# Attention beside a feed-forward layer: partial PV sums and the start of the other matmul groups

## The chip, the cores and the metric

The kernel runs on one core of one Trainium2 chip. The metric is the device time of one execution in microseconds. Three runs of the kernel before gave 674.62, 674.64 and 674.77 us; their median is 674.64 us.

## The reference

One input `x` of 2048 tokens by 640 features goes through a layer norm. Two branches then read the normalised tokens, and the output is the sum of the input and both branches:

```
xn = layernorm(x)
q = xn @ wq            # 32 heads of 20
k, v = xn @ wk, xn @ wv   # one head, shared by all 32
o = softmax(q k^T / sqrt(20)) @ v
h = relu(xn @ w1 + b1) ** 2     # 1536 wide
out = x + o @ wo + h @ w2 + b2
```

All tensors are bf16. By far the largest piece is the softmax: 32 heads by 2048 queries by 2048 keys of exponentials.

## The kernel before

**Tiling.** The 2048 queries are cut into four chunks of 512 and the 32 heads into eight groups of four, so that there are 32 blocks (line `NBLK`). A block has 16 key tiles of 128. A block and a key tile give four units, one for each head: a QK product of 20 rows by 128 keys by 512 queries that fills one PSUM bank. The four heads of a group use four different row strips of TensorE, so one batch of up to four QK matmuls runs side by side (line 1397).

**Two ways to an exponential.** ScalarE takes two or three units in one ACTIVATE of 1024 or 1536 columns (line 1678, tile PT). VectorE takes units one at a time (line 1777, tile pbx): it adds a constant, rounds to int16 and so makes an approximate exponential by bit pattern. A key tile that goes this way needs four such instructions and three copies of the result with an added phase of 32, 64 or 96; these are made by VectorE (line 1798) or in pieces by GpSimd (line 1860). A ScalarE tile then costs one step of the PV sum, a VectorE tile four.

**PV.** A step of PV is four matmuls of 32 output columns in four column strips (line 1991). All steps of a block add up in one PSUM bank. When the sum is complete, VectorE copies it to SBUF (line 2051), the softmax sum goes through three small DMAs, and the block is divided and packed for the output product.

**The other groups.** Feed-forward, query projection and output groups are sums in PSUM too, of 5 to 18 steps of four matmuls (line 1015, functions `groups` and `u_FFN`, `u_OUT`, `u_QP`). There are 48 feed-forward groups, 19 query groups and 32 output groups. Each has a place in units of blocks at which it is due. VectorE reads each result.

**PSUM.** There are eight banks. In most of the kernel banks 0 to 4 belong to ScalarE's units (three and two in turn), and banks 5, 6 and 7 (`MREG`, line 91) are shared by the open PV sum, the open group of the other kind, and VectorE's QK units. If none of the three is free for VectorE, bank 2 can be lent to it (lines 1485 to 1492), and then ScalarE's batch has two units in place of three.

**Order of the work.** The order of each engine's queue is made at build time by a list scheduler (class `Sched`, line 264). Streams (QK, exponentials, VectorE's tiles, PV, the other groups) offer their next instruction with a priority, and the scheduler issues by its own account of when engines and banks come free. A table `PLAN` (line 95) has 64 rows, one for each half block, with thresholds and with a seed; `pick` (line 1373) uses the seed to choose at some steps between small variants, as other lead times or one unit fewer. Everything on the chip then waits on semaphores in that fixed order.

**What sets the start of a PV sum and of a group.** `PVblk` (line 1937) runs the PV sum of one block. With `MX = 0` (line 186) it opens as soon as one step is ready (`SEG0 = 1`). For blocks 2 to 28 a sum may be cut once (`SEGS = 2`) where only one step is waiting, at least 8 are done and at least 8 are left (line 1983). The part is then added up in SBUF by `evict` (line 2022), its bank is given back, and the next part opens when 4 steps wait, or earlier if the buffers of exponentials fill up (`SEGR` PT slots of 24 or `SEGP` pbx buffers of 10). `due` (line 2163) lets a group of the other kinds start when it is one block late (`mlate`), or up to two blocks early (`mearly`) if no more than 4 PV steps are waiting (`mq`). It does not ask whether a PV sum is open.

Of the kernel before, what the change touches and what calls it, by code (L numbers as in the profile page):

```python
# [159 lines left out]
)]  # L160
PAAT = 24.7
PAQ = ()
NPX = 1
# [22 lines left out]
MX, MXL, MXP, MXE = 0, 1.0, 0, 1.0  # L186
# [19 lines left out]
PVEND = 0.5  # L206
# [3 lines left out]
PVU = 0.8  # L210
# [314 lines left out]
def bass_parallel_sum__grouped_kv_mqa__dense_activation_squared_relu__prompt_kernel(nc, A_x, A_wq, A_wk, A_wv, A_wo, B_x, B_w1, B_b1, B_w2, B_b2, out):  # L525
    es = ExitStack()
    with es:
# [77 lines left out]
        sc = Sched()  # L605
# [762 lines left out]
        def plan(name):  # L1368
            return spot[1][name]
# [937 lines left out]
```

## Time and profile before

| what | value |
|---|---|
| median of three runs | 674.64 us |
| profiled execution, its own time | 675.58 us |
| its span, first to last instruction | 673.8 us |
| TensorE clock granted | full over the whole span |
| ScalarE busy | 655.6 us, 97% |
| VectorE busy | 616.6 us, 92% |
| TensorE, pipelined ends modelled | 663.5 us, 98% |
| GpSimd busy | 464.1 us, 69% |
| DMA, mean | 45 GB/s |

The span is the time between the first and the last instruction of the trace, so the profiled execution has 1.8 us around it. A busy TensorE is not TensorE at its peak, since matmul ends overlap in the trace; the spacing of starts tells more. `PEld` are weight loads, which run beside the matmuls. The idle time in a row is that of the engine just before the instructions of that row, followed by what ended it.

### The profile page before, as it was taken

To read this page: it belongs to the slowest core of one execution; us is meant where nothing else is said; L and a number is where in the kernel's file an instruction comes from. 1 tells how busy PE (TensorE), PEld (TensorE's weight loads), DVE (VectorE), ACT (ScalarE), POOL (GpSimd) and SP (SyncE) were. 2 spreads that over 40 slices of the span, in tenths; PEclk is the share of its full clock that TensorE was granted. 3 is DMA by queue.
4 is the path that set the end of the run, shared out by engine and by line. 5 is a ranking of instruction groups with operands and counts; after the bars stand their busy time and mean duration, and the time that the engine had idled before them with its cause. 6 is when DMAs were issued, how large, how long until landed. Compare 5 with 4: busy or idle time off the path is not lost.

```text
span 673.8 us, 23427 instructions
## 1 busy us (share of the span) xinstructions
PE 663.5 (98%) x9828; PEld 225.5 (33%) x9828; DVE 616.6 (92%) x1114; ACT 655.6 (97%) x664; POOL 464.1 (69%) x808
## 2 busy tenths in 40 slices
PE   8999999999999999999999999999999999999998
PEld 6332222222223333332322333332233333333334
DVE  7988999999998898989999898889999998998897
ACT  6999999999999999999999999999999999999994
POOL 2657777867777777778878577776766777776700
PEclk9999999999999999999999999999999999999999
DMA  9441222311111111110111111120110011111001
GB/s 262 129 71 46 52 60 72 83 45 38 25 24 32 34 44 38 27 45 18 25 30 28 45 43 27 29 51 19 31 31 20 20 44 45 38 38 32 22 2 42
DMA packets 39914, 30.43 MB, mean 45 GB/s; under 512 B 22817, under 2 KB 34818, under 8 KB 39810
## 3 DMA queue, kind: packets, MB, share of 16 engines
q1 hardware_dynamic: 39810, 28.93, 18.2%
q8 instruction: 79, 1.29, 0.8%
q14 instruction: 25, 0.20, 0.1%
HBM read 11.49 MB, written 2.62 MB: 21 GB/s over the span
## 4 chain that ended last, share of the span: by engine, by line
PE 64%; ACT 19%; DVE 15%; DMA 1%; issue 1%; POOL 0%
PE ps L1991 24%; PE ps L1397 20%; PE ps L1015 19%; ACT PT L1678 19%; DVE pbx L1777 8%; DVE stats L743 2%; DVE pbx L1798 1%; DVE hT_tmp L1151 1%; DMA dn<-Tn 1%; DMA pbx<-in_A_x_dram 0%; DVE big L1159 0%; DVE Tn L2051 0%; DVE qpk L1106 0%; DVE OTs L2067 0%; DVE xnT L958 0%
## 5 line engine op out<-in xcount | busy, mean ns | idle before, releaser
L1678 ACT ACTIVATE PT<-ps 128x1024 bf16<-128x1024 f32 (+1 forms) x641 | 649.4, 1163 | 3.9 <-PE ps L1397 3.3
L1860 POOL INT64_ADD pbx<-pbx x767 | 445.3, 600 | 158.5 <-DVE pbx L1798 84.2
L1777 DVE TENSOR_SCALAR pbx<-ps 128x512 int16<-128x512 f32 x629 | 413.7, 686 | 40.4 <-PE ps L1397 37.1
L1397 PE MATMUL ps<-qT,kT 20*128 20x512 bf16 x2048 | 250.8, 384 | 3.5 <-DVE pbx L1777 2.0
L1991 PE MATMUL ps<-pbx,vp 128*32 128x512 bf16 x1896 | 174.4, 383 | 0.2 <-POOL pbx L1860 0.2
L1397 PEld LDWEIGHTS ps<-qT,kT 20*128 20x128 bf16 x2048 | 63.0, 91 | 241.6 <-ACT PT L1678 156.7
L1991 PE MATMUL ps<-PT,vx 128*32 128x512 bf16 x1416 | 135.9, 383 | 0.1
L1015 PE MATMUL ps<-xnT,w_sb 128*32 128x512 bf16 x960 | 72.9, 383 | 0.2
L1015 PE MATMUL ps<-w_sb,big 128*32 128x320 bf16 x1536 | 72.1, 301 | 0.1
L1798 DVE TENSOR_SCALAR pbx<-pbx 128x2048 int16<-128x2048 int16 x102 | 69.1, 689 | 0.3
L1991 PEld LDWEIGHTS ps<-pbx,vp 128*32 128x32 bf16 x1896 | 46.5, 95 | 56.5 <-issue 35.3
L1991 PE MATMUL ps<-pbx,vx 128*32 128x512 bf16 x632 | 61.2, 383 | 0.0
L1991 PEld LDWEIGHTS ps<-PT,vx 128*32 128x32 bf16 x1416 | 36.3, 95 | 42.5 <-issue 31.3
L1015 PEld LDWEIGHTS ps<-w_sb,big 128*32 128x32 bf16 x1536 | 34.1, 96 | 25.4 <-issue 17.9
L1151 DVE TENSOR_SCALAR hT_tmp<-ps,b1col 128x512 bf16<-128x512 f32 x48 | 35.6, 742 | 2.3 <-PE ps L1015 2.3
L1015 PE MATMUL ps<-wo_p,OTp 128*32 128x320 bf16 (+1 forms) x608 | 31.8, 302 | 0.1
L1015 PE MATMUL ps<-xnT,wq_sb 128*32 128x512 bf16 x375 | 29.0, 383 | 0.2 <-DVE pbx L1777 0.2
L1015 PEld LDWEIGHTS ps<-xnT,w_sb 128*32 128x32 bf16 x960 | 19.2, 95 | 26.9 <-issue 16.5
L794 POOL TENSOR_SCALAR big<-pbx,rstd,nmr 128x640 bf16<-128x640 bf16 x16 | 14.0, 892 | 15.4 <-DVE nmr L783 13.9
L1991 PEld LDWEIGHTS ps<-pbx,vx 128*32 128x32 bf16 x632 | 16.4, 95 | 18.0 <-issue 11.8
L2067 DVE TENSOR_TENSOR OTs<-Tn,Rb 128x512 bf16<-128x512 f32 x29 | 20.3, 699 | 0.0
L1159 DVE TENSOR_TENSOR big<-hT_tmp 128x512 bf16<-128x512 bf16 x48 | 20.0, 421 | 0.1
(95 smaller groups left out, 191.4 us busy)
## 6 DMA issues: line engine op xcount, KB each, us to landing
Rb<-kT SPq DMA_DIRECT2D x29, 256.0 KB
xres<-in_A_x_dram SPq DMA_DIRECT2D x16, 160.0 KB
out_dram<-out_sb SPq DMA_DIRECT2D x16, 160.0 KB
qT<-qpk SPq DMA_DIRECT2D x105, 20.0 KB
OTp<-OTs SPq DMA_DIRECT2D x105, 20.0 KB
pbx<-in_A_x_dram SPq DMA_DIRECT2D x3, 640.0 KB
w_sb<-in_B_w_dram SPq DMA_DIRECT2D x1, 1920.0 KB
w_sb<-in_B_w_dram SPq DMA_DIRECT2D x12, 160.0 KB, 2.4
```

The lines of the kernel that those rows point to most:

```text
L743: v = yield (lambda hh=hh: Req(("dve", 400.0, 470.0, [lambda e: e.bn_stats(out=stats6[:, st, hh, :], in_=x_sb[:, st, 320 * hh:320 * hh + 3 ...
L794: alts = [("dve", 400.0, 440.0, [lambda e: e.tensor_scalar(out=xn(st), in0=x_sb[:, st, :], scalar1=rstd[:, st:st + 1], scalar2=nmr[:, st:s ...
L1015: return lambda e: e.matmul(ps[32 * j:32 * j + m, b_[0], 0:n], Lj, R, start=first, stop=last, tile_position=(0, 32 * j))
L1151: v = yield Req(("dve", 658.0, 742.0, [lambda e: e.tensor_scalar(out=hT_tmp[:, k, :], in0=ps[:, b_[0], :], scalar1=b1col[:, f:f + 1], scal ...
L1159: w = yield Req(("dve", SQ_D, SQ_D + 82.0, [lambda e: e.tensor_tensor(out=h2(qc, f), in0=hT_tmp[:, k, :], in1=hT_tmp[:, k, :], op=ALU.mult)]),
L1397: ins.append(lambda e, i=i, b=b, t=t, h=h: e.matmul(ps[:, i, :], kT[32 * h:32 * h + DH, t * 128:(t + 1) * 128], qT[32 * h:32 * h + DH, b % ...
L1678: op = yield Req(("act", d_, d_ + 107.0, [lambda e, slot=slot, n=n, src=src: e.activation(out=PT[:, slot:slot + n, :], in_=ps[:, src, :], ...
L1777: return Req(("dve", d_, d_ + 82.0, [lambda e: e.tensor_scalar(out=PB[:, k, hsl, :], in0=ps[:, bk:bk + np_, :], scalar1=OFFS, scalar2=0.0, ...
L1798: return Req(("dve", 600.0, 684.0, [lambda e: e.tensor_scalar(out=PB[:, k, :, :], in0=PB[:, s, :, :], scalar1=PH_D[j], scalar2=None, op0=A ...
L1860: return lambda e: e.int64_add(PB8[:, k, c0 // 4:c1 // 4], PB8[:, s, c0 // 4:c1 // 4], int(PH_D[j]) * 0x0001000100010001)
L1991: ins = [(lambda e, h=h, first=first, last=last: e.matmul(ps[32 * h:32 * h + 32, bk, :], lhs, rhs[h], start=first, stop=last, tile_positio ...
L2067: w = yield Req(("dve", NM_D, NM_D + 82.0, [lambda e: e.tensor_tensor(out=dst[:, :], in0=Tn[:, tb, :], in1=Rb[:, a, :], op=ALU.mult)]), (l ...
```

## The change

The matmuls, formulas and buffers stay. What changes is when a PV sum is cut, when it opens, and when a group of the other kinds may start.

- `MX` goes from 0 to 1. `due` then asks whether a PV sum of blocks 2 to 28 is open. While one is open, a group starts only if it is 0.2 blocks late (`MXL`). While none is open the old rule holds.
- A PV sum may have three parts (`SEGS = 3`). A cut still needs that only one step is waiting; it now needs 5 steps done and 5 left (`SEGM`), and `m_near()`: a group of the other kinds is open, or one of the next six has its inputs and is due within one block (`MXE`).
- The opening of a part is no longer withheld. In two cases it is offered 200 ns (`SEGW`) after TensorE comes free in the scheduler's account, so that other ready work goes ahead: while a group of the other kinds is open (the first opening of a block excepted), and while `m_near()` holds and fewer than 8 steps wait (`SEG0`, `SEGK`). Both end when 18 PT slots (`SEGR`) or 8 pbx buffers (`SEGP`) are taken. In the kernel before, the first of the two was not active with `MX = 0`, and the second withheld the second part until 4 steps waited.
- The seeds and some thresholds of 56 of the 64 rows of `PLAN` are others. With `broken`, `DLEAD`, `ringhi`, `dstarv` and `DMAXR` a few half blocks choose banks, lead times and the number of VectorE units per batch in another way. In the kernel before 46 rows have a seed, after it 50.

```diff
@@ -93,70 +93,70 @@
-    (640, 3500.0, 600.0, 6000.0, 0, 900.0, 14, 2, 0.0, 3, 60.0, 600, 4.0, 2000.0, 2, 0.3, 0, 0.0, 400.0, 4, 0.5, 2, (0, 3, 400.0, 300.0), 1, 329933548, 2, 1.0, 2.0, 4, 99, 2000.0, -1, 400.0, 600.0, 560),
...
+    (640, 3500.0, 600.0, 4000, 300, 900.0, 12, 2, 0.0, 3, 60.0, 600, 4.0, 2000.0, 2, 0.3, 0, 0.0, 0.0, 4, 0.5, 1, (0, 3, 400.0, 300.0), 1, 231792246, 3, 1.0, 2.0, 4, 99, 2000.0, -1, 400.0, 600.0, 560),
...
@@ -183,8 +183,9 @@
-MX, MXL, MXP, MXE = 0, 1.0, 0, 1.0
-SEGS, SEG0, SEGK, SEGM, SEGR, SEGP = 2, 1, 4, 8, 16, 8
+SEGW = 200.0
+MX, MXL, MXP, MXE = 1, 0.2, 0, 1.0
+SEGS, SEG0, SEGK, SEGM, SEGR, SEGP = 3, 8, 8, 5, 18, 8
@@ -1947,10 +1948,11 @@
                     def poll():
+                        low = False
                         if si == 0 and split and MX and seg + i and any(len(h) > 1 for h in held) and sum(slot_busy) < SEGR and sum(r.last is None for r in pbres) < SEGP:
-                            return None
+                            low = True
                         if si == 0 and split and (not MX or m_near()) and len(pv_items[b]) < min(SEGK if seg else SEG0, pv_total[b] - i) and sum(slot_busy) < SEGR and sum(r.last is None for r in pbres) < SEGP:
-                            return None
+                            low = True
                         best = None
@@ -1989,7 +1991,7 @@
-                        return Req(("pe", ...), ..., "PV", mode="col", cols=512.0)
+                        return Req(("pe", ...), ..., "PV", mode="col", cols=512.0, after=sc.free["pe"] + SEGW if low else 0.0)
```

The functions that read these names, as they stand in both kernels:

```python
        def m_near():
            return any(len(h) > 1 for h in held) or any(u[0] <= pos() + plan("mshift") + MXE and have(*u[3]) for u in units[:6])
...
            if MX and any(2 <= k_ < NBLK - NLAST for k_ in pvbank):
                return d >= MXL
            return d >= plan("mlate") or d >= -plan("mearly") and sum(len(v) for k_, v in pv_items.items() if PVG == 0 or k_ in pvbank) <= plan("mq")
```

More of the change, by code (lines that the diff above doesn't have):

```diff
@@ L1991, in poll @@
                         ins = [(lambda e, h=h, first=first, last=last: e.matmul(ps[32 * h:32 * h + 32, bk, :], lhs, rhs[h], start=first, stop=last, tile_position=(0, 32 * h))) for h in range(HPG)]
-                        return Req(("pe", PE512, PE512 + PELAT, ins), dd + (bank[bk].last if first else []), (PVEND if cur_a[0] == NSB else PVU if sum(slot_busy) >= plan("ringhi") + pick("P%d_%d" % (b, i), 0, 0, -4, 4) else 1) - (MXP if split else 0) if b == min(pvbank, default=b) else 1.1, "PV", mode="col", cols=512.0)
+                        return Req(("pe", PE512, PE512 + PELAT, ins), dd + (bank[bk].last if first else []), (PVEND if cur_a[0] == NSB else PVU if sum(slot_busy) >= plan("ringhi") + pick("P%d_%d" % (b, i), 0, 0, -4, 4) else 1) - (MXP if split else 0) if b == min(pvbank, default=b) else 1.1, "PV", mode="col", cols=512.0, after=sc.free["pe"] + SEGW if low else 0.0)
                     cur = [None, None, False]
```

110 rows, old and new, of the table PLAN are left out of this document.

## The prediction

> **What bounds the kernel now.** I read the page first: busy shares, the chain, the costliest groups.
>
> ```profile
> span 673.8 us, 23427 instructions
> PE 663.5 (98%) x9828; PEld 225.5 (33%) x9828; DVE 616.6 (92%) x1114; ACT 655.6 (97%) x664; POOL 464.1 (69%) x808
> PE 64%; ACT 19%; DVE 15%; DMA 1%; issue 1%; POOL 0%
> L1678 ACT ACTIVATE PT<-ps 128x1024 bf16<-128x1024 f32 (+1 forms) x641 | 649.4, 1163 | 3.9 <-PE ps L1397 3.3
> L1777 DVE TENSOR_SCALAR pbx<-ps 128x512 int16<-128x512 f32 x629 | 413.7, 686 | 40.4 <-PE ps L1397 37.1
> L1397 PE MATMUL ps<-qT,kT 20*128 20x512 bf16 x2048 | 250.8, 384 | 3.5 <-DVE pbx L1777 2.0
> L1991 PE MATMUL ps<-pbx,vp 128*32 128x512 bf16 x1896 | 174.4, 383 | 0.2 <-POOL pbx L1860 0.2
> L1991 PE MATMUL ps<-PT,vx 128*32 128x512 bf16 x1416 | 135.9, 383 | 0.1
> L1015 PE MATMUL ps<-xnT,w_sb 128*32 128x512 bf16 x960 | 72.9, 383 | 0.2
> L1015 PE MATMUL ps<-w_sb,big 128*32 128x320 bf16 x1536 | 72.1, 301 | 0.1
> L1798 DVE TENSOR_SCALAR pbx<-pbx 128x2048 int16<-128x2048 int16 x102 | 69.1, 689 | 0.3
> L1991 PE MATMUL ps<-pbx,vx 128*32 128x512 bf16 x632 | 61.2, 383 | 0.0
> L1015 PE MATMUL ps<-wo_p,OTp 128*32 128x320 bf16 (+1 forms) x608 | 31.8, 302 | 0.1
> L1015 PE MATMUL ps<-xnT,wq_sb 128*32 128x512 bf16 x375 | 29.0, 383 | 0.2 <-DVE pbx L1777 0.2
> ```
>
> ScalarE is idle for only 3.9 us ahead of its exponentials. VectorE is idle for 673.8 − 616.6 = 57.2 us, and 37.1 of these end with a QK matmul: VectorE has no unit to work on. So ScalarE sets the time, and it gets shorter only if it has fewer instructions or if VectorE takes over units. The second view, stretches of the span, says when VectorE starves. Three calls stand here one after the other: the edges and the middle; six stretches with many output groups (first row and sum, 290 us); five with mostly feed-forward groups (first row and sum, 250 us). The columns are PE, PEld, DVE, ACT and POOL busy.
>
> ```profile
> 0.00:20.00 20.00, 17.41 (x191) 11.82 (x191) 15.78 (x64) 14.80 (x28) 8.06 (x27) 1.00 0.93 285
> 20.00:660.00 640.00, 635.50 (x9407) 207.37 (x9404) 592.02 (x1030) 637.00 (x634) 456.08 (x782) 1.00 0.17 38
> 660.00:674.00 14.00, 10.54 (x242) 6.31 (x234) 8.82 (x22) 3.78 (x5) 0.00 (x0) 1.00 0.14 49
> ...
> 200.00:250.00 50.00, 48.58 (x764) 17.02 (x764) 45.10 (x76) 49.95 (x50) 37.47 (x69) 1.00 0.16 39
> ...
> sum 290.00, PE 287.89 PEld 102.11 DVE 258.59 ACT 289.85 POOL 215.88; mean PE 47.98 PEld 17.02 DVE 43.10 ACT 48.31 POOL 35.98
> ...
> 100.00:150.00 50.00, 50.00 (x671) 14.36 (x672) 49.99 (x88) 49.85 (x52) 37.35 (x61) 1.00 0.27 67
> ...
> sum 250.00, PE 247.77 PEld 74.88 DVE 241.56 ACT 248.68 POOL 185.99; mean PE 49.55 PEld 14.98 DVE 48.31 ACT 49.73 POOL 37.20
> ```
>
> Between 20 and 660 us ScalarE has 3.0 us idle in 640, VectorE 48.0. The output stretches have 290 − 258.6 = 31.4 us of it, the feed-forward ones 250 − 241.6 = 8.4 us. In both an open PV sum and an open group take two of banks 5 to 7; an output group keeps its bank longest (17 or 18 steps).
>
> The third view is the timeline, for what a QK batch costs TensorE.
>
> ```profile
> 299.74 0.39 PE L1397 MATMUL ps<-qT,kT 20*128 20x512 bf16 x3
> ...
> 300.06 0.40 PE L1991 MATMUL ps<-PT,vx 128*32 128x512 bf16 x4
> ...
> 300.40 0.40 PE L1397 MATMUL ps<-qT,kT 20*128 20x512 bf16 x4
> ...
> 300.72 0.61 PE L1991 MATMUL ps<-pbx,vp 128*32 128x512 bf16 x8
> ...
> 306.98 0.39 PE L1015 MATMUL ps<-xnT,w_sb 128*32 128x512 bf16 x4
> ...
> 309.23 0.74 DVE L1151 TENSOR_SCALAR hT_tmp<-ps,b1col 128x512 bf16<-128x512 f32 x1
> ...
> 667.91 1.81 PE L1015 MATMUL ps<-w_sb,big 128*32 128x320 bf16 x48
> ```
>
> Two PV steps in a row are 0.61 − 0.40 = 0.21 us apart. A QK batch, with three rows or four, starts 0.34 us after a PV step and is followed by the next 0.32 us later: it takes 0.32 + 0.34 − 0.21 = 0.45 us. Output steps are (1.81 − 0.30) / 11 = 0.137 us apart (twelve steps, 0.30 the length of one matmul in the page's row). Each of the 641 ACTIVATEs has its own QK batch, so TensorE needs 641 × 0.45 = 288 us for QK, (1896 + 1416 + 632) / 4 = 986 PV steps × 0.21 = 207, (960 + 375) / 4 × 0.21 = 70 for feed-forward and query steps and (1536 + 608) / 4 × 0.137 = 73 for output steps: 638 us, nearly all of the span. So three engines are full together, and a batch holds only 2048 / 641 = 3.2 of four possible rows.
>
> **The change part by part.** *Groups of the other kinds wait while a PV sum is open.* A feed-forward group keeps its bank from its first step at 306.98 to the end of its copy at 309.97 us, 3.0 us. If the PV sum's bank is free in that time, VectorE has two of the three shared banks in place of one; batches get their fourth row, and bank 2 is lent less often. Two terms follow.
>
> First, ScalarE. Its forms, with VectorE's copies of PV sums:
>
> ```profile
> L1678 ACT ACTIVATE PT<-ps 128x1024 bf16<-128x1024 f32 x505 | 487.3, 1073 | 3.7 <-PE ps L1397 3.3
> L1678 ACT ACTIVATE PT<-ps 128x1536 bf16<-128x1536 f32 x135 | 202.6, 1500 | 0.2
> L2051 DVE COPY Tn<-ps 128x512 f32<-128x512 f32 x27 | 18.4, 680 | 0.0
> L2024 DVE COPY Tn<-ps 128x512 f32<-128x512 f32 x2 | 1.4, 679 | 0.0
> ```
>
> A unit costs 1500 − 1073 = 427 ns. Of the 1073 ns, 1073 − 2 × 427 = 219 belong to no unit, and instructions overlap by (641 × 1163 ns − 649.4 us) / 641 = 150 ns, so one instruction fewer saves 69 ns. ScalarE has 505 × 2 + 135 × 3 + 1 = 1416 units; in strict turns of three and two they would make 1416 / 2.5 = 566 instructions. I take half of the way, 604: 37 × 69 ns = **2.6 us** saved on ScalarE (call it s; ends 5.2 at 566, and a loss of 4.6 at 708, all in pairs). The same 37 batches give TensorE 37 × 0.45 = 17 us of room.
>
> [...]
>
> Second, VectorE's idle time. If output stretches became as dense as feed-forward ones, 31.4 − 290 × 8.4 / 250 = 21.6 us would be won. If every wait for a QK matmul went, 37.1. I take the middle, **29.4 us**. The other end is below nothing: groups that start late bunch up and hold banks back to back; −10 us is my bound, an estimate: two stretches that are full now (50.0 busy) become as starved as the one at 200 us (45.1).
>
> *PV sums are cut into up to three parts.* Each cut adds one VectorE instruction of 0.68 us (the row of L2024; the later ones add from PSUM at the 680 ns of the copies). Now there are 2 of them. 27 blocks may be cut, so the ends are none and 54 − 2 = 52 more, 35.4 us. A cut asks that one step is left waiting. Now TensorE serves other groups first and PV lags, hence only 2; after the change PV runs with no group beside it and should drain more often. I take between one cut a block (27) and one and a half (40): 33, or 31 more, 31 × 0.68 = **21.1 us**. It lies on the path: VectorE is one of the full engines, and nothing hides it but the idle time just counted. The bank goes back only after this copy; VectorE's queue is in order, so a QK unit behind it starts 0.68 us later, which its second bank now covers. If that cover is missing, the next QK batch is late, then ScalarE.
>
> *How both sum up.* With g = 29.4 − 21.1 = 8.3 us of VectorE time won, whole key tiles move from ScalarE to VectorE until both end together. A tile takes 4 × 649.4 / 1416 = 1.83 us from ScalarE and gives VectorE 4 × 413.7 / 632 + 102 / 158 × 0.68 = 3.06 us (2048 − 1416 = 632 units are 158 tiles). With k tiles the time falls by s + 1.83 k on ScalarE and by g − 3.06 k on VectorE; both agree at a fall of (3.06 s + 1.83 g) / 4.89 = (8.0 + 15.2) / 4.89 = **4.7 us**. k is 1.2, and its three more PV steps each cost TensorE 1.2 × 3 × 0.21 = 0.8 us, far below the 17 us of room.
>
> *Opening offers 200 ns later, other limits.* A part that stands back by 0.2 us, less than one QK batch, costs only where ScalarE's tiles stay in PT; with 18 slots taken the rule is off. I put it at 0, between −1 and +1 us, five such delays that reach ScalarE, or five that let a QK batch go first. *The due rule of 0.2.* A block lasts 640 / 31 = 20.6 us, so a group may start 4.1 us late. What waits for it are the query tiles (asked for 1.9 blocks ahead), the next chunk's feed-forward buffers and the outputs: hidden at 0; if it fails, a block of QK waits for its query tile. SP issues the same DMAs in the same order of blocks; each block's three small ones follow the last part alone, so nothing new is queued there. *Seeds.* They reorder steps; start (0 to 20) and tail (660 to 674) can move too. No row bounds this; I take 0 and put ±1.5 us, a tenth of the tail's length, into the range.
>
> The profiled execution took 675.58 us with its span of 673.8, and the median is 674.64, 0.14% lower. The fall of 4.7 us taken from the median gives **669.9 us**.
>
> **The rivals.** *Cuts cost more than they free* (slower). Three parts in every block (52 more, 35.4 us) and only the 21.6 us of the output stretches won: g = −13.8, and with s = 2.6 the time rises by 3.5 us to 678.1. It decides from g = −4.3 on, that is from 26 us or 38 more cuts. For it: VectorE is at 92% already. Against it: PV lags behind a full TensorE, which keeps the backlog up. [...]
>
> *The change does not do what it says.* TensorE has 638 us of work, so groups are always 0.2 blocks late and start beside an open sum as now. Then few cuts come (8, 5.4 us), little idle goes (6 us) and s is 0.7: a fall of 0.7 us, 674.0. For it speaks the full TensorE; against it that a group may start two blocks early once a sum is cut.
>
> *More than forecast.* All 37.1 us of waits go, one cut a block (25 more, 17.0 us), strict turns (s = 5.2): g = 20.1, a fall of 10.8 us, 663.9. For it: the 2.5 units per instruction are what banks 0 to 4 are laid out for. Against: two banks for VectorE and ScalarE's turns both fill batches from the same four rows.
>
> **How the numbers follow.** Forecast 0.50, more than forecast 0.20, no effect 0.11, slower 0.19. The range 663 to 678 reaches to both outer cases and leaves about half of the slower one out, and the little below 663. About 0.2%, 1.3 us, is what a measurement can tell from no change. The first two cases are faster, and a quarter of the third with its seeds: 0.73. Same is most of the third, 0.07; slower 0.20. The likeliest case's own range is 666 to 673.
>
> **What would show it.** Right: some 33 evictions at L2024; fewer than 620 ACTIVATEs with over 200 of them 1536 wide; waits of L1777 for QK near 10 us; VectorE near 95%; some 640 units at L1777. Wrong: over 40 evictions with fewer units at L1777 (slower), or fewer than 10 evictions and L1678 as now (no effect). It would also be wrong if ScalarE got gaps ahead of its exponentials, from late query tiles or from a starved QK batch.

## The result and the profile after

The changed kernel takes 682.86 us (682.69 to 683.1, three runs) against 674.64 us: 1.0122 of the time before, with a 95% interval of 1.0099 to 1.0145. It is 8.2 us slower. The forecast was 4.7 us faster, and the time lies 4.9 us above the range.

The page of the changed kernel: busy shares, and the two groups that answer to those of before. All lines of the kernel lie one to two lower.

```profile
span 681.4 us, 23472 instructions
PE 668.1 (98%) x9858; PEld 227.1 (33%) x9858; DVE 620.5 (91%) x1115; ACT 658.6 (97%) x665; POOL 454.5 (67%) x808
L1679 ACT ACTIVATE PT<-ps 128x1024 bf16<-128x1024 f32 (+1 forms) x642 | 652.4, 1180 | 7.2 <-PE ps L1398 5.9
L1778 DVE TENSOR_SCALAR pbx<-ps 128x512 int16<-128x512 f32 (+1 forms) x620 | 408.6, 686 | 45.1 <-PE ps L1398 41.9
```

Its groups with shapes kept apart, and the copies of PV sums (L2026 are the cuts, L2053 the ends of blocks):

```profile
L1679 ACT ACTIVATE PT<-ps 128x1024 bf16<-128x1024 f32 x502 | 485.5, 1089 | 5.9 <-PE ps L1398 5.4
L1679 ACT ACTIVATE PT<-ps 128x1536 bf16<-128x1536 f32 x140 | 211.0, 1508 | 1.3 <-PE ps L1398 0.5 <-PE ps L1993 0.2
L2026 DVE COPY Tn<-ps 128x512 f32<-128x512 f32 x5 | 3.4, 685 | 0.6 <-PE ps L1993 0.5
L2026 DVE TENSOR_TENSOR Tn<-ps,Tn 128x512 f32<-128x512 f32 x2 | 1.4, 680 | 0.0
```

The same stretches as before: the sum of the six output stretches, then that of the five feed-forward ones.

```profile
sum 290.00, PE 287.15 PEld 100.80 DVE 257.61 ACT 288.77 POOL 202.86; mean PE 47.86 PEld 16.80 DVE 42.93 ACT 48.13 POOL 33.81
...
sum 250.00, PE 246.35 PEld 73.44 DVE 237.61 ACT 248.32 POOL 190.44; mean PE 49.27 PEld 14.69 DVE 47.52 ACT 49.66 POOL 38.09
```

Almost nothing that was forecast is there. There are 7 cuts, not 33. The ACTIVATEs are 642, not 604, so no batch was saved. VectorE waits 41.9 us for QK matmuls, more than the 37.1 of before, and not the 10 or so of the forecast. Its output stretches are as thin as before (257.6 of 290 us busy, 258.6 then), and the feed-forward ones became thinner (237.6 of 250, 241.6 then). ScalarE has 502 × 2 + 140 × 3 = 1424 units, so VectorE has 624, 8 fewer than the 632 of before. With these eight units more, ScalarE's exponentials are busy for 652.4 − 649.4 = 3.0 us longer, and its idle time ahead of them is 7.2 in place of 3.9 us, 3.3 us more. Together that is 6.3 of the 7.6 us by which the span grew. The other 1.3 us lie behind the last exponential, which ends 10.1 us before the end of the span in the kernel before and 11.3 us in the changed one.

### The profile page after: what moved, and what is told of

Read it like the earlier page. It is cut to its first block, busy times and chain, and to the rows that moved or that the text cites. A ratio compares the mean times of both kernels' runs of the same rounds, so it can differ in the third digit from the quotient of the medians.

```text
span 681.4 us, 23472 instructions
## 1 busy us (share of the span) xinstructions
PE 668.1 (98%) x9858; PEld 227.1 (33%) x9858; DVE 620.5 (91%) x1115; ACT 658.6 (97%) x665; POOL 454.5 (67%) x808
## 4 chain that ended last, share of the span: by engine, by line
PE 61%; ACT 28%; DVE 10%; issue 0%; DMA 0%
ACT PT L1679 28%; PE ps L1993 23%; PE ps L1398 19%; PE ps L1016 18%; DVE pbx L1778 4%; DVE stats L744 1%; DVE pbx L1799 1%; DVE hT_tmp L1152 1%; DMA pbx<-in_A_x_dram 0%; DVE vp L1068 0%; DVE Tn L2053 0%; DVE big L1160 0%; DVE xnT L959 0%; DVE mv L747 0%; DVE kT L1040 0%
## 5 line engine op out<-in xcount | busy, mean ns | idle before, releaser
L1679 ACT ACTIVATE PT<-ps 128x1024 bf16<-128x1024 f32 (+1 forms) x642 | 652.4, 1180 | 7.2 <-PE ps L1398 5.9
L1861 POOL INT64_ADD pbx<-pbx x767 | 435.5, 587 | 169.7 <-DVE pbx L1799 87.8
L1778 DVE TENSOR_SCALAR pbx<-ps 128x512 int16<-128x512 f32 (+1 forms) x620 | 408.6, 686 | 45.1 <-PE ps L1398 41.9
L1993 PE MATMUL ps<-pbx,vp 128*32 128x512 bf16 x1872 | 172.3, 383 | 1.1 <-POOL pbx L1861 0.8
L1993 PE MATMUL ps<-PT,vx 128*32 128x512 bf16 x1424 | 137.9, 384 | 1.7 <-ACT PT L1679 0.9
L1799 DVE TENSOR_SCALAR pbx<-pbx 128x2048 int16<-128x2048 int16 x107 | 72.7, 689 | 0.3
L1993 PEld LDWEIGHTS ps<-PT,vx 128*32 128x32 bf16 x1424 | 36.5, 95 | 47.1 <-issue 33.7
L1016 PEld LDWEIGHTS ps<-xnT,w_sb 128*32 128x32 bf16 x960 | 19.4, 95 | 27.2 <-issue 16.3
```

Of the source, the lines that this page charges most:

```text
L1016: return lambda e: e.matmul(ps[32 * j:32 * j + m, b_[0], 0:n], Lj, R, start=first, stop=last, tile_position=(0, 32 * j))
L1679: op = yield Req(("act", d_, d_ + 107.0, [lambda e, slot=slot, n=n, src=src: e.activation(out=PT[:, slot:slot + n, :], in_=ps[:, src, :], ...
L1778: return Req(("dve", d_, d_ + 82.0, [lambda e: e.tensor_scalar(out=PB[:, k, hsl, :], in0=ps[:, bk:bk + np_, :], scalar1=OFFS, scalar2=0.0, ...
L1799: return Req(("dve", 600.0, 684.0, [lambda e: e.tensor_scalar(out=PB[:, k, :, :], in0=PB[:, s, :, :], scalar1=PH_D[j], scalar2=None, op0=A ...
L1861: return lambda e: e.int64_add(PB8[:, k, c0 // 4:c1 // 4], PB8[:, s, c0 // 4:c1 // 4], int(PH_D[j]) * 0x0001000100010001)
L1993: ins = [(lambda e, h=h, first=first, last=last: e.matmul(ps[32 * h:32 * h + 32, bk, :], lhs, rhs[h], start=first, stop=last, tile_positio ...
```

## The experiments

Two theories stood against each other. **R**: the new rules for cuts and starts cost the time, and the other numbers of the plan rows only shuffle the order. **F**: the rows of each kernel are fitted to the exact order in which its scheduler arrives at them; what matters is that fit, and the rules as such matter little. The prediction had put the rows at ±1.5 us.

**The two halves of the change, each alone.** First the rows of the changed kernel under the old rules; then the new rules with the rows of before. Compared place by place, 61 of the 64 rows differ between the two kernels.

```diff
 PLAN = [...]      # rows_alone: all 64 rows as in the changed kernel
 MX, MXL, MXP, MXE = 0, 1.0, 0, 1.0
 SEGS, SEG0, SEGK, SEGM, SEGR, SEGP = 2, 1, 4, 8, 16, 8
```

> The kernel before with the 64 plan rows of the changed kernel, its rules for PV sums and groups untouched. Theory R (the new rules cost the 8.2 us, the rows only shuffle the order): near 674.6 us, at most 677. Theory F (rows fit only the order that they were chosen for, and any other rule turns them into a random choice): slower than both kernels, over 684 us.

```diff
 PLAN = [...]      # rules_alone: all 64 rows as in the kernel before
 SEGW = 200.0
 MX, MXL, MXP, MXE = 1, 0.2, 0, 1.0
 SEGS, SEG0, SEGK, SEGM, SEGR, SEGP = 3, 8, 8, 5, 18, 8
```

> The changed kernel with the 64 plan rows of before. Theory R: near 682.9 us, the whole loss with the rules alone, between 680 and 685. Theory F: over 684 us, slower than the changed kernel, since the rows of before no longer fit.

They took 693.2 and 692.1 us beside 675.3 for the kernel before (ratios 1.0268, interval 1.022 to 1.0315, and 1.0252, 1.0222 to 1.0281). Each half alone is slower than both whole kernels. R falls: the old rules with other rows lose 18 us, where it expected 677 at most. F expected over 684 us for both. A wait row of rows_alone (us in total, times, longest) shows where VectorE loses:

```profile
DVE pbx L1777 <- PE ps L1397: 67.3, 135, 2.3
```

VectorE waits 67.3 us for QK matmuls against 37.1 before, on the same rules. A smaller part of this run's loss is TensorE's clock, which the last section comes to: its two runs took 694.5 us with a mean granted clock of 0.992 and 691.9 with 0.998.

**Both rules without any fit.** All 64 rows are the commonest one, without a seed.

```diff
+    (640, 3500.0, 600.0, 6000.0, 0, 900.0, 12, 2, 0.0, 3, 60.0, 600, 4.0, 2000.0, 2, 0.3, 0, 0.0, 0.0, 4, 0.5, 2, (0, 3, 400.0, 300.0), 1, 0, 8, 1.0, 2.0, 4, 99, 2000.0, -1, 400.0, 600.0, 560),
...
```

> The kernel before with all 64 plan rows set to the row that is commonest among them, without a seed: what the old rules give when no row is fitted. Theory R: some us over 674.6, and the pair of this and the next run stands 8 us apart. Theory F: 680 us or more, 5 us or more over the kernel before, and the next run within 4 us of it.

> The changed kernel with the same 64 plain rows as the run of the old rules. Theory R: 8 us over that run, as 682.9 stands over 674.6. Theory F: within 4 us of it, in either direction.

The old rules took 687.4 us, the new ones 688.9: 1.4 us between them. The loss of the change stands at 8.2, so most of it is not seen where no row is fitted. Each side is one order here, and the four refitted kernels below differ by up to 4.0 us under the same rules, so 1.4 is no more than an indication. Seen from here, the rows of before are worth 12.8 us to the old rules (687.4 to 674.6) and those of the changed kernel 6.0 us to the new ones.

**One row's seed.** This asks how far a row's effect reaches. In the kernel before, one row gets another seed.

```diff
-    (..., 1, 483735196, 4, 1.0, ...),     # row 4
+    (..., 1, 1, 8, 1.0, ...),
```

> The kernel before with one number pair changed: the seed of plan row 4 (483735196 with nz 4 becomes 1 with nz 8), which is read while block 2's second half and block 3's place in the order are made; all rules and the other 63 rows as before. If rows work each on its own half block, the time stays within 2 us of 675. If each row was fitted to the state that the rows ahead of it leave (theory F), all later rows lose their fit: over 682 us, like the run with the other kernel's rows.

```diff
-    (..., 1, 959505964, 4, 1.0, ...),     # row 60
+    (..., 1, 1, 8, 1.0, ...),
```

> The same with the seed of plan row 60, which is read in the last two blocks (959505964 with nz 4 becomes 1 with nz 8). Theory F: little is left behind it that could lose its fit, so within 3 us of 675. If any change of a seed costs the same wherever it lies: as much as the run with row 4.

Row 4, read while the exponentials are in the first half of block 2, takes the kernel to 694.1 us (1.0281, 1.0237 to 1.0326). Row 60, read in block 30 (the last is 31), makes 676.2 (1.0016, 1.0003 to 1.003), both beside 675.0 for the kernel before. This one number early in the plan costs 19 us, more than twice the whole change; the one near the end costs 1.2 us. That the early one costs more because all later rows meet another state than the one they were chosen for is F's reading. Two rows fit it and do not prove it. The sparser work shows on VectorE:

```profile
L1777 DVE TENSOR_SCALAR pbx<-ps 128x512 int16<-128x512 f32 x598 | 393.1, 683 | 61.3 <-PE ps L1397 58.7
```

That is row4_seed: VectorE has 32 units fewer (ScalarE has 502 × 2 + 148 × 3 = 1448) and waits 58.7 us for QK.

**What VectorE's time costs in a fixed order.** The order of every engine stays that of before; only 25 copies are added, which the scheduler does not know of.

```diff
+        spare = sb("spare", [128, 368], BF16)
...
-            v = yield Req(("dve", 600.0, 682.0, [lambda e: e.tensor_copy(out=Tn[:, tb, :], ...
+            v = yield Req(("dve", 600.0, 682.0, ([lambda e: e.tensor_copy(out=spare[:, :], in_=ps[:, pvb, 0:368])] if seg == 0 and b >= 2 else []) + [lambda e: e.tensor_copy(out=Tn[:, tb, :], ...
```

> The kernel before in its own order on every engine, with one more VectorE copy out of PSUM (368 columns to an unused tile) ahead of the copy of the finished PV sum in 25 of the blocks 2 to 28: some 0.5 us each, 13 us in all. It measures what VectorE time costs while nothing is replanned. If VectorE's time is on the path, as the prediction's g term has it: 5 to 13 us more, 680 to 688. If its 57 us of idle time take it up: under 677.

It took 683.9 us beside 675.0 (1.013, 1.0087 to 1.0174). In the view of line 2051 and on its page:

```profile
L2051 DVE CAST spare<-ps x25: 523/530/540, 87.9 to 614.7; 128x368 bf16<-128x368 f32 x25
...
L1678 ACT ACTIVATE PT<-ps 128x1024 bf16<-128x1024 f32 (+1 forms) x641 | 654.4, 1143 | 7.4 <-PE ps L1397 5.4
L1777 DVE TENSOR_SCALAR pbx<-ps 128x512 int16<-128x512 f32 x629 | 413.0, 685 | 39.9 <-PE ps L1397 36.5
```

The copies are 25 × 0.53 = 13.3 us, and 8.9 us of it reach the end, two thirds. VectorE's 57 us of idle time take up only a third, and its waits for QK stay (36.5 us). ScalarE has the same 1416 units, yet its idle time grows by 3.5 us and its busy time by 5.0: its instructions start later into the one before, and lost overlap counts as busy (641 × 1.163 − 649.4 = 96 us of overlap before, 641 × 1.143 − 654.4 = 78 us here). So the prediction was right that VectorE's time lies on the path. In a fixed order it weighs 0.67, not the 0.37 (1.83 / 4.89) that it had with tiles shifted. One thing is not kept apart: each copy stands ahead of the one that gives the PV bank back, so it also holds that bank 0.53 us longer.

**More separation.** In the order of the changed kernel, `due` still lets 66 of the 86 groups of blocks 2 to 28 start beside an open PV sum; before it was 84 of 88, and 73 of 88 in plain_new_rules. On plain rows the next kernel makes it 26 of 90, with 31 cuts. By the first matmul in TensorE's queue, which comes later, it is 42 of 90 (70 of 88 in plain_new_rules).

```diff
-MX, MXL, MXP, MXE = 1, 0.2, 0, 1.0
+MX, MXL, MXP, MXE = 1, 1.0, 0, 1.0
...
-... and len(pv_items[b]) == 1 and si + 1 >= SEGM ...
+... and len(pv_items[b]) <= 4 and si + 1 >= SEGM ...
...
-            return d >= plan("mlate") or d >= -plan("mearly") and sum(...) <= plan("mq")
+            return d >= plan("mlate") or d >= -plan("mearly") and (MX and not pvbank or sum(...) <= plan("mq"))
```

> The changed kernel with the 64 plain rows (beside the run plain_new_rules, 688.9 us) and the separation made to work: a PV sum is cut where up to 4 steps wait (not only 1), a group beside an open sum must be a whole block late (not 0.2), and without an open sum the number of waiting steps does not hold it. In its order 26 of 90 groups of blocks 2 to 29 begin beside an open PV sum, 73 of 88 in plain_new_rules. The prediction's mechanism (a second shared bank for VectorE): waits of L1778 for QK fall from some 40 us to under 25, fewer ACTIVATEs with more of 1536, and the time falls by 5 us or more to below 684. The rival (those banks are not what VectorE lacks): waits stay over 35 us, time within 5 us of 688.9 or above.

It took 688.2 us, beside 688.9 of plain_new_rules. Its groups, and then those of plain_new_rules:

```profile
L1679 ACT ACTIVATE PT<-ps 128x1024 bf16<-128x1024 f32 x470 | 463.8, 1108 | 3.7 <-PE ps L1398 3.3
L1778 DVE TENSOR_SCALAR pbx<-ps 128x512 int16<-128x512 f32 x588 | 385.1, 682 | 44.2 <-PE ps L1398 39.2 <-PE ps L1993 1.9
L1679 ACT ACTIVATE PT<-ps 128x1536 bf16<-128x1536 f32 x169 | 257.3, 1536 | 1.1 <-PE ps L1398 0.8
```

```profile
L1679 ACT ACTIVATE PT<-ps 128x1024 bf16<-128x1024 f32 x529 | 508.2, 1079 | 5.3 <-PE ps L1398 4.4 <-PE ps L1993 0.7
L1778 DVE TENSOR_SCALAR pbx<-ps 128x512 int16<-128x512 f32 x594 | 388.9, 682 | 43.6 <-PE ps L1398 39.9 <-PE ps L1993 1.5
L1679 ACT ACTIVATE PT<-ps 128x1536 bf16<-128x1536 f32 x126 | 189.1, 1509 | 1.8 <-PE ps L1398 1.2
```

One half of the mechanism is there: bank 2 is lent less, 169 ACTIVATEs are 1536 wide against 126, and there are 639 of these two forms against 655. The other half is not: VectorE waits as long for QK as without it (39.2 against 39.9 us), the 24 further cuts take 24 × 0.68 = 16.3 us of VectorE, and it ends with 600 units, 12 fewer. The gain and the price cancel, within what two unfitted orders can tell.

How far does this variant free a bank? The kernels give the order of TensorE's and VectorE's queues, and the traces the times. Between 40 and 640 us an open PV sum and an open group hold banks at once in the share of the time that the table gives. A wait is here all idle time of VectorE that ends with a unit whose QK batch came last, slightly more than the pages count.

| kernel | both hold a bank | waits for QK in that time, us | waits in the rest, us |
|---|---|---|---|
| before | 50% | 23.5 | 14.0 |
| changed kernel | 50% | 26.6 | 15.7 |
| plain_new_rules | 48% | 19.0 | 23.2 |
| separated | 38% | 13.3 | 28.6 |

So the change itself freed almost no bank, and this variant frees one in only a tenth of the time. In that tenth the waits did not go, they moved: separated has 28.6 of its 41.9 us while at most one of the two holds a bank. On plain rows a wait is no likelier beside both than beside one (19.0 us in 290, 23.2 in 310). In the kernel before it is (23.5 us in 303, 14.0 in 297). If all its time were like its better half, 23.5 − 303 × 14.0 / 297 = 9 us would go, an estimate. The lack of a bank can then be a part of the waits, far below the 29.4 us that the prediction put on it.

**Rows fitted anew to both rules by the same effort.** Starting from the plain rows, some thousand trials each changed one row's seed, and a trial was kept if the scheduler's own account of the end improved. Two sequences of trials for each rule.

```diff
-    (..., 1, 0, 8, 1.0, ...),     # 6 to 12 of the 64 plain rows
+    (..., 1, <seed>, <nz>, 1.0, ...),
```

> The old rules with rows fitted anew: from the 64 plain rows, some thousand trials of another seed in one row at a time, a trial kept if the list scheduler's own account of the end became earlier; 12 rows got a seed. Theory F (what a plan row is fitted to makes the time; the rules as such make 2 us or less): 5 us or more under plain_old_rules (687.4), and the new rules fitted by the same effort end within 4 us of the old ones. Theory R (the new rules as such cost 8 us): the new ones end 6 us or more above, in both pairs.

> The same with another sequence of trials; 7 rows got a seed. Theory F: 5 us or more under plain_old_rules, within 3 us of the first. Theory R: the same, as both keep the old rules.

> The new rules with rows fitted anew by the same effort from the same plain rows; 6 rows got a seed. Theory F: 4 us or more under plain_new_rules (688.9) and within 4 us of the old rules' fitted kernels. Theory R: 6 us or more above them.

> The same with another sequence of trials; 12 rows got a seed. Theory F: as the run before, and at or under the changed kernel (682.9), whose rows were fitted to the same rules. Theory R: 6 us or more above the old rules' fitted kernels.

The old rules took 684.3 and 685.2 us, the new ones 687.2 and 683.3: means of 684.8 and 685.2. The rules cannot be told apart, and the two kernels of the new rules alone lie 4.0 us apart. Over the three pairs (plain and refitted) the new rules come out 0.8 us slower on average, where R asks for 8. In the profiled executions, plain_old_rules and both refits of the old rules contain a stretch at half the TensorE clock (mean granted clock 0.996, 0.997 and 0.997), 3.4 us long in plain_old_rules, and the kernels of the new rules none (1.000 in all three; the second run of new_rules_fit1 has 0.995). That can have cost the old rules up to 1.7 us each, an estimate (half of 3.4, taken for all three), so the new rules may be up to 2 us worse than this average says. The fit gained less than F asked of the old rules: 3.1 and 2.2 us under plain_old_rules, not 5, and 1.7 and 5.6 for the new ones. new_rules_fit2 ends at 683.3, not under the changed kernel.

All kernels together; the last column adds busy and idle time of the exponentials' row. Measured again beside the experiments, the kernel before took 674.6 to 675.3 us. VectorE's units are 2048 less ScalarE's.

| kernel | us | VectorE units | cuts | ScalarE, us |
|---|---|---|---|---|
| before | 674.6 | 632 | 2 | 653.3 |
| row60_seed | 676.2 | 628 | 2 | 654.9 |
| changed kernel | 682.9 | 624 | 7 | 659.6 |
| new_rules_fit2 | 683.3 | 620 | 9 | 661.5 |
| copied_twice | 683.9 | 632 | 2 | 661.8 |
| old_rules_fit1 | 684.3 | 620 | 3 | 662.3 |
| old_rules_fit2 | 685.2 | 624 | 2 | 663.5 |
| new_rules_fit1 | 687.2 | 620 | 10 | 663.7 |
| plain_old_rules | 687.4 | 612 | 3 | 665.5 |
| separated | 688.2 | 600 | 31 | 666.8 |
| plain_new_rules | 688.9 | 612 | 7 | 666.4 |
| rules_alone | 692.1 | 612 | 7 | 669.9 |
| rows_alone | 693.2 | 604 | 9 | 673.3 |
| row4_seed | 694.1 | 600 | 5 | 673.5 |

The time follows ScalarE's stretch, and this roughly follows how many units VectorE could take and how often ScalarE's next batch was late. It does not follow the rules. This says where the time lies and not why: the exponentials fill the span but for some 11 us at the start and 8 to 11 at the end.

## Why the prediction was wrong

Two steps failed. The mechanism (a PV sum and the other groups kept apart, which frees a bank for VectorE) did not come about. And the term that then decided, the rows, was put at nothing.

**What bounds the kernel** held in part. ScalarE sets the time, VectorE's time is on the path (copied_twice), and each unit that VectorE does not take comes back on ScalarE. That TensorE is the third full engine stayed a sum (638 us) that no run tested by itself.

**The term of 21.1 us for cuts** was wrong in its count: 5 more, not 31. A cut asks that only one step waits; with up to four allowed, and the other two edits, separated had 31. The rival "does not do what it says" had this right with 8 cuts, and with ACTIVATEs as before; its 674.0 us missed because it too put the rows at nothing. The reason that it gave, a full TensorE, was not tested. The price per cut, 0.68 us of VectorE, held.

**The term of 29.4 us of VectorE's idle time** failed. With 66 of 86 groups still let start beside an open sum, and both holding banks in 50% of the time as before, the rule does not separate. The waits grew by 4.8 us in place of falling by 29.4. The prediction read a wait for a QK matmul as the lack of a bank, and the difference between stretches as what a bank would win. No row showed either. In separated, which gave the bank back for a tenth of the time, the waits stayed, and the kernel before bounds the gain at some 9 us. What the rest of the waits come from stays open.

**The term s, 2.6 us from wider ACTIVATEs**, did not come in the changed kernel (642 in place of 604). Separation on plain rows gave 15 fewer (640 against 655 in plain_new_rules).

**Seeds, "No row bounds this; I take 0 and put ±1.5 us",** is the step that decided. One seed moved the time by 19 us and a full set of rows by 17 to 18. So this edit to the scheduler's rules could not leave the rows' part at zero: under the new rules the rows of before lose 17 us, and what the new rows reach is a matter of their own fit. The 8.2 us are, on plain rows, 1.4 for the rules, and the rest is that the rows of before fit better (12.8 us) than those of the change (6.0). These parts depend on each other, as rules_alone and rows_alone show, so they are a bookkeeping and no law. That the missing part is fit, and not a bound that the new rules set to any fit, is argued from the equal refits and not shown: whether the new rules could reach 674 us with better rows stays open.

**The slower rival** gave 678.1 for another reason, 52 cuts. The changed kernel is slower with 5 more. The prediction's last sign of being wrong, gaps ahead of ScalarE's exponentials, did come: 7.2 us against 3.9.

## What to carry to other kernels

Where a list scheduler with fitted seeds makes the order, first measure what one seed is worth: change one early and one late, and compare. If that is larger than the effect of a rule, the rule is to be judged with rows fitted equally for both sides, or with none. And a wait for a matmul on a full TensorE isn't yet a lack of PSUM banks (in separated both sums held a bank for 38% of the time in place of 48%, and VectorE's waits were 39.2 us in place of 39.9): free the bank, measure in how much of the time it became free, and look whether the wait goes.

## What the runs showed of the hardware

All of this was measured on this case's kernels: granted clock and pauses are those of the traces of their profiled executions. TensorE's clock fell to half in the middle of the execution of four kernels: once each in plain_old_rules, old_rules_fit1 and old_rules_fit2, three times in rows_alone (mean clock 0.992). The half clock behind the last matmuls is left aside here; in the kernel before the last matmul ends at 670.5 us, and the clock is 0.94 from 674 to 676 us. In plain_old_rules, around the late arrival of a softmax denominator by DMA, VectorE's queue waits 1.54 us, and the QK batches behind it come late:

```profile
90.05 0.69 DVE L2067 TENSOR_TENSOR OTs<-Tn,Rb 128x512 bf16<-128x512 f32 x1 [1.54 <-DMA Rb<-kT]
...
91.39 0.40 PE L1991 MATMUL ps<-pbx,vx 128*32 128x512 bf16 x4 [1.33 <-DVE pbx L1777]
...
92.16 1.02 ACT L1678 ACTIVATE PT<-ps 128x1024 bf16<-128x1024 f32 x1 [1.25 <-PE ps L1397]
```

Stretches of two us of the same kernel; the third column from the right is the granted clock:

```profile
90.00:92.00 2.00, 0.67 (x10) 0.20 (x6) 1.95 (x4) 0.90 (x1) 0.79 (x2) 1.00 0.28 70
92.00:94.00 2.00, 2.00 (x25) 0.45 (x23) 2.00 (x4) 1.84 (x2) 2.00 (x4) 0.82 0.22 63
94.00:96.00 2.00, 2.00 (x18) 0.35 (x14) 1.77 (x5) 1.12 (x2) 1.36 (x3) 0.50 0.15 29
96.00:98.00 2.00, 2.00 (x24) 0.45 (x22) 0.98 (x3) 1.69 (x2) 1.59 (x3) 0.83 0.26 74
```

The pause was 1.33 us, and the clock fell at 93.3 us, when matmuls ran again: 0.18, 0.50 and 0.17 of the three stretches from 92 to 98 us were lost, 1.7 us in all, which is 3.4 us at half. In rows_alone, with a clock of 0.98 from 100 to 200 and again from 200 to 400 us, matmuls took longer from near 180, 214 and 378 us on: four took 0.65 and 0.64 us in place of 0.40, and eight 1.01 in place of 0.61. TensorE's longest pause in the 2.7 us ahead was 0.95, 0.44 and 0.58 us. In old_rules_fit1, where eight matmuls take 0.71 us near 468 us, the pause ahead was 1.80 us. In old_rules_fit2 the clock is 0.91 from 80 to 100 us, and TensorE was idle there for 20 − 18.70 = 1.30 us in all. In the kernel before a pause of 1.23 us (from 154.53 us) was followed by no half clock: it has 1.00 in each two us from 150 to 160.

So the half clock followed pauses of 0.44 to 1.80 us, and a pause of 1.23 us passed without it. The length of a pause alone does not say whether the clock falls, and what does was not shown. The changed kernel and the kernel before had a mean granted clock of 1.000 in their profiled executions, so this has no part in the 8.2 us. It is a part of what rows_alone, plain_old_rules and the two refits of the old rules lose, up to 1.7 us for each fall by the estimate above.
